# Fused causal attention and two expert layers: the attention stage rewritten as a pipeline over heads with one written order for TensorE

## Chip, cores and metric

One core of a Trainium2 chip. The metric is the device time of one execution in microseconds (us). The kernel before took 442.41 us, the median of three runs from 440.71 to 443.2.

## The reference

Inputs: q, k, v of 2 batches, 8 heads, 576 rows and 64 columns, and a vector s per head. For each head:

```python
scores = scale * np.matmul(q, k.transpose(0, 1, 3, 2))
cum = np.cumsum(np.maximum(s, 0.0), axis=-1)
bias = -(cum[:, :, :, None] - cum[:, :, None, :])
scores = np.where(causal, -1000000000.0, scores + np.minimum(bias, 0.0))
scores = scores - np.max(scores, axis=-1, keepdims=True)
attn = np.exp(scores)
attn = attn / (np.sum(attn, axis=-1, keepdims=True) + 1e-09)
return np.matmul(attn, v)
```

The 1152 rows of 512 that come out go through a layer of 8 experts (top one by a gate, with a capacity), and its result through a second layer of 8 experts with another gate and a bias. The change touches the attention stage alone.

## The kernel before, in words

**Tiling.** Heads are worked in eight pairs p (two heads i = 0, 1 of one batch b, pair hp of four). The 576 query rows of a head are cut into five tiles t of 64, 128, 128, 128 and 128 rows (`ROWS`, starting at `QS`); tile t sees keys 0 to w = 64, 192, 320, 448 or 576. Tile 0 is called the 64-row tile.

**Operands, `load(p)` (L272 to L311).** One transfer brings q and k of a pair, transposed, into `qkd`, twice over the 128 partitions; others bring rows of the cumulated s into `kb` and `qb` and the values into `vt`. A score is made of rounded numbers and their remainders: ScalarE casts q to `qa` and k to `ka` (L306, L308), VectorE casts q to the upper half of `qb` (L307), and GpSimd (VectorE for the first pair) subtracts to get the remainders `qa` and `kb` (L309, L310). `load(p + 1)` is called at the start of pair p. The transfers are issued on SyncE's queue; `qkd`, `qa` and `ka` have two buffers, as have `qb` and `kb`.

**Scores (L355 to L377).** For each head and tile, TensorE makes `ps` out of two products, `qa` by `ka` (L364) and `qb` by `kb` (L366), and adds the causal mask on the diagonal block as a bfloat16 product of an identity and a matrix `later` (L369). Tile 4, 576 wide, is made in two halves of 288, in two PSUM banks. Each bank holds one piece. VectorE reads it, scales it and takes the running minimum (L372) into `sc` (three buffers); ScalarE takes the exponential and its row sum (L376) into `ebuf[t, i]`.

**Transposes (L378 to L387).** TensorE turns the exponentials in blocks of 128 columns (L383) into PSUM tiles `pt`, and VectorE (L385) or ScalarE (L387) copies them to `eT`. For the second head of a pair both copies of tile 4 are ScalarE's. The 64-row tile is turned as a 64-row block.

**Values and rows (L434 to L483).** When both heads are turned, TensorE multiplies the values by `eT` into `pa` (columns 0 to 320) and `pb` (320 to 576), the two heads in the two halves of the columns of the array (L441). ScalarE and VectorE copy them to `xu`; ten products with an identity and the gate's weights (L454) turn them into rows `px`; VectorE scales these by the inverse row sums (L457, L467), and SyncE stores them to `x1` (`keep_rows`). Pairs 4 and 7 also route their batch (`route`).

**PSUM.** `pss` has four banks for `ps`, `pst` four for `pt`, `pa`, `pb`, `px` and the router's tiles.

**Order.** The program is written tile by tile, but a scheduler chooses the order on each engine by what it thinks is ready; that order is then fixed. So scores of a pair come to stand among transposes and value products of the one before. `tc.issue_after(x)` makes the instructions under it come after x in that order, `tc.keep_in_program_order` and `behind` keep an instruction's place. The expert layers that follow have an order written by hand; the first of their gathers reads the stored rows.

Of the kernel before, what the change touches and what calls it, by code (L numbers as in the profile page):

```python
# [6 lines left out]
F32 = mybir.dt.float32  # L7
# [10 lines left out]
NT = 5  # L18
# [63 lines left out]
def build(tc, ctx, spots, tab, qk, v, s, wg, wa, cap, mod, wg2, mb, wb, out):  # L82
# [108 lines left out]
    with ExitStack() as actx:  # L191
# [13 lines left out]
        later = ae.tile([P, P], BF16, name="later")  # L205
        nc.gpsimd.memset(later, 0.0)
        nc.gpsimd.affine_select(out=later, in_=later, pattern=[[-1, P]], compare_op=ALU.is_ge, fill=-8.0e9,
                                base=0, channel_multiplier=1)
# [10 lines left out]
        for t in range(NT):  # L219
            for j in range(2):  # L220
                et = ae.tile([P, P * (t + 1)], F32, name=f"e{t}_{j}")
                nc.gpsimd.memset(et[:, 64 + P * t:P * (t + 1)], 0.0)
                ebuf[t, j] = et
# [48 lines left out]
        def load(p):  # L272
# [8 lines left out]
            vt = ap.tile([P, NT, 2 * D], F32, name="vt")  # L281
# [37 lines left out]
        ahead = load(0)  # L319

        for b in range(B):
            for hp in range(4):
                p = 4 * b + hp
                qa2, ka2, qb2, kb2, vt = ahead
                if p < 7:
                    ahead = load(p + 1)
                if p == 0:
                    with tc.issue_after(operands[-1]):
                        nc.gpsimd.memset(wgid[:, :, P:DW], 0.0)
                        filled = nc.gpsimd.tensor_copy(wgid[:, :, 0:P], ident.unsqueeze(1).to_broadcast([P, 4, P]))  # L330
                    behind(ctab, tab)
                    wgv = wg.rearrange("(hp two d) e -> two d hp e", two=2, d=D)
                    for i in range(2):
                        behind(wgid[64 * i:64 * i + 64, :, P + E * i:P + E * i + E], wgv[i])
                if p > 3:
                    for i in range(2):
                        first.append(fetch(wa, 0, 2 * (p - 4) + i, pin=True))
                if p == 3:
                    for i in range(2):
                        xc = const.tile([H1, 2, RW], F32, name=f"xc{i}")  # L340
                        with tc.issue_after(filled.ins):
                            nc.gpsimd.memset(xc, 0.0)
                        xcs.append(xc)
                    zrow = ac.tile([P, 1, DM], F32, name="zrow")
                    with tc.issue_after(filled.ins):
                        nc.gpsimd.memset(zrow, 0.0)
                    tc.keep_in_program_order(nc.sync.dma_start(
                        out.rearrange("(p t) d -> p t d", t=9), zrow.to_broadcast([P, 9, DM])))
                eTs = []
                for i in range(2):  # L350
                    h = 2 * hp + i
                    qa, ka, qb, kb = qa2[:, i], ka2[:, i], qb2[:, i], kb2[:, i]
                    eT = ap.tile([P, NT, S], F32, name="eT", bufs=3)
                    eTs.append(eT)
                    for t in range(NT):  # L355
                        r = ROWS[t]
                        w = QS[t] + r
                        q0 = QS[t]
                        sc = ap.tile([P, S], F32, name="sc", bufs=3)
                        low = 3.0e38  # L360
                        for c0, c1 in ((0, w // 2), (w // 2, w)) if w > 512 else ((0, w),):
# [100 lines left out]
                if p == 7:  # L462
                    exp = route(1)
# [743 lines left out]
```

## Time and profile before

| what | value |
|---|---|
| median of 3 runs | 442.41 us |
| the profiled execution | 439.67 us |
| its span, first to last instruction | 437.9 us |
| TensorE busy (matmul) | 411.4 us, 94% |
| VectorE busy | 198.6 us, 45% |
| ScalarE busy | 170.5 us, 39% |
| GpSimd busy | 130.4 us, 30% |
| mean granted TensorE clock | 0.973 |

Times in the trace count from the first instruction of the span. Busy shares are means over all stages: attention, about the first 125 us, and the expert layers after it. [...] L12 is line 12 of the kernel before.

### The profile page before, as it was taken

The page shows a single profiled execution, that of the slowest core. Times are in us where ns is not written, and L with a number is a line of the kernel's source. Part 1 is how long each engine was busy: PE and PEld are TensorE (multiplying, and loading weights), DVE is VectorE, ACT ScalarE, POOL GpSimd, SP SyncE. Part 2 cuts the span into 40 slices and gives each one's busy share as a digit, 9 for nine tenths or more (in the row PEclk, how much of TensorE's full clock was granted, in tenths as well). Part 3 has the DMA queues.
Part 4 walks back from the last instruction along what each step waited for, and adds up shares of the span by engine and source line. Part 5 has one row for each costly group of instructions (what it writes and reads, how often), then busy time and mean ns, then how long its engine had stood idle before and what let it go on. Part 6 is the DMA issues. An engine that isn't in the chain of part 4 may idle for free.

```text
span 437.9 us, 8869 instructions
## 1 busy us (share of the span) xinstructions
PE 411.4 (94%) x3193; PEld 371.9 (85%) x3193; DVE 198.6 (45%) x782; ACT 170.5 (39%) x452; POOL 130.4 (30%) x154
## 2 busy tenths in 40 slices
PE   4997999999987999999999999999999999999980
PEld 1775777788757999998999999998999999999980
DVE  7779878998671032232322315176912243111110
ACT  5776888876531121212121212146313364131220
POOL 4397444330018220020110100323464447030120
PEclk8889999999998999999999999999999999999995
DMA  3846279343324766676768696994149646010010
GB/s 113 309 115 207 75 252 325 100 158 127 102 107 128 248 194 209 198 241 210 252 201 294 189 305 208 271 310 160 36 108 361 214 135 207 21 40 16 7 41 23
DMA packets 30580, 74.64 MB, mean 170 GB/s; under 512 B 9196, under 2 KB 11628, under 8 KB 30526
## 3 DMA queue, kind: packets, MB, share of 16 engines
q1 hardware_dynamic: 24190, 66.75, 45.8%
q0 software_dynamic: 6336, 7.22, 6.0%
q8 instruction: 27, 0.44, 0.4%
q14 instruction: 27, 0.22, 0.2%
HBM read 63.78 MB, written 10.51 MB: 170 GB/s over the span
## 4 chain that ended last, share of the span: by engine, by line
PE 58%; DVE 5%; DMA 3%; issue 2%; ACT 1%; POOLq 0%; POOL 0%; DVEq 0%
PE ps L657 32%; PE ps L665 6%; PE ps L667 6%; PE ps L666 6%; PE pty L732 3%; PE ptx L642 2%; PE p L748 1%; DMA st<-in_wb 1%; DMA yc<-y,idx 1%; DVE lo L577 1%; DVE pos L173 1%; DMA xc<-x,list 1%; DVE hidden L723 0%; ACT hi L575 0%; POOLq L835 0%
## 5 line engine op out<-in xcount | busy, mean ns | idle before, releaser
L657 PE MATMUL ps<-xn,st 128*128 128x160 f32 (+7 forms) x576 | 83.6, 299 | 0.0
L657 PE MATMUL ps<-hidden,st 128*128 128x160 f32 (+7 forms) x576 | 81.8, 296 | 0.0
L657 PEld LDWEIGHTS ps<-xn,st 128*128 128x128 f32 x576 | 77.7, 193 | 1.9 <-ACT yT L709 1.1
L657 PEld LDWEIGHTS ps<-hidden,st 128*128 128x128 f32 x576 | 76.3, 190 | 0.6
L710 DVE COPY yT<-ps 128x276 f32<-128x276 f32 (+8 forms) x26 | 9.2, 353 | 98.6 <-ACT yT L709 98.6
L376 ACT ACTIVATE e<-sc,nmx 64x64 f32<-64x64 f32 (+4 forms) x80 | 44.6, 560 | 15.2 <-DVE sc L372 8.3
L364 PE MATMUL ps<-ka,qa 128*64 128x64 f32 (+2 forms) x96 | 35.8, 380 | 6.4 <-DVE qa L309 4.5
L709 ACT COPY yT<-ps 128x276 f32<-128x276 f32 (+8 forms) x26 | 8.2, 316 | 79.1 <-PE ps L657 48.7
L665 PE MATMUL ps<-hidden,hi 128*128 128x276 f32 x128 | 38.2, 299 | 0.6 <-DVE hidden L723 0.6
L665 PE MATMUL ps<-xs,hi 128*128 128x276 f32 x128 | 38.4, 300 | 0.0
L601 POOL DMA_INDIRECT xc<-x,idx x14 | 13.9, 994 | 80.3 <-DVE eq L770 77.4
L383 PE MATMUL pt<-ident,e 128*128 128x128 f32 (+1 forms) x240 | 36.8, 282 | 1.0 <-DVE eT L385 0.9
L666 PE MATMUL ps<-hidden,hi 128*128 128x276 f32 x128 | 37.1, 290 | 0.2 <-DVE hidden L723 0.2
L666 PE MATMUL ps<-xs,hi 128*128 128x276 f32 x128 | 37.1, 290 | 0.0
L667 PE MATMUL ps<-hidden,lo 128*128 128x276 f32 x128 | 37.1, 290 | 0.0
L667 PE MATMUL ps<-xs,lo 128*128 128x276 f32 x128 | 37.1, 290 | 0.0
L372 DVE TENSOR_SCALAR_CACHE_REDUCE sc<-ps 64x64 f32<-64x64 f32 (+4 forms) x80 | 32.9, 422 | 6.8 <-PE ps L369 3.9
L309 POOL TENSOR_TENSOR qa<-qkd,qb 64x576 fp32r<-64x576 f32 x14 | 20.5, 1462 | 38.8 <-ACT qa L306 38.2
L577 POOL TENSOR_TENSOR lo<-st,hi 128x512 fp32r<-128x512 f32 x16 | 22.3, 1401 | 32.7 <-ACT hi L575 32.6
L824 POOL DMA_INDIRECT out<-yr,oi x13 | 15.6, 1201 | 53.8 <-ACT yr L733 49.2
L383 PEld LDWEIGHTS pt<-ident,e 128*128 128x128 f32 (+1 forms) x240 | 26.9, 143 | 4.9 <-DVE eT L385 1.1
L366 PE MATMUL ps<-kb,qb 128*64 128x64 f32 (+2 forms) x96 | 29.1, 310 | 0.6 <-POOL kb L310 0.6
(275 smaller groups left out, 779.8 us busy)
## 6 DMA issues: line engine op xcount, KB each, us to landing
st<-in_wa SPq DMA_DIRECT2D x64, 512.0 KB
st<-in_wb SPq DMA_DIRECT2D x24, 512.0 KB
qkd<-in_qk SPq DMA_DIRECT2D x6, 1152.0 KB
y<-yr SPq DMA_DIRECT2D x8, 390.0 KB
vt<-in_v SPq DMA_DIRECT2D x8, 320.0 KB
qkd<-in_qk SPq DMA_DIRECT2D x4, 576.0 KB
out<-zrow SPq DMA_DIRECT2D x1, 2304.0 KB
x<-xrow SPq DMA_DIRECT2D x2, 768.0 KB
```

The source lines that it names most:

```text
L309: eng.tensor_tensor(qa[64:128, i], qd[64:128], qb[64:128, i].bitcast(F32), op=ALU.subtract)
L364: nc.tensor.matmul(o, qa[:, q0:q0 + r], ka[:, c0:c1], start=True, stop=False, skip_group_check=True)
L366: nc.tensor.matmul(o, qb[:, q0:q0 + r], kb[:, c0:c1], start=False, stop=c1 <= q0, skip_group_check=True)
L372: nc.vector.tensor_scalar(sc[:r, c0:c1], o, -0.125, low, op0=ALU.mult, op1=ALU.min, accum_out=nmx[:r])
L376: nc.scalar.activation(e[:r, :w], sc[:r, :w], AF.Exp, bias=nmx[:r], scale=-1.0, accum_out=rsum[:r, b, t, h:h + 1])
L383: nc.tensor.transpose(pt[:, j - g0, :r], e[:r, j * P:(j + 1) * P], ident[:r, :r])
L577: eng.tensor_tensor(lo[:, c:c + h], st[:, c:c + h], hi[:, c:c + h].bitcast(F32), op=ALU.subtract)
L657: pin(nc.tensor.matmul(out[:, 0:c], w[:, o:o + P], mv, start=first, stop=last, skip_group_check=True))
L665: pin(nc.tensor.matmul(out[:, 0:c], hi, mv[:, 0, :], start=first, stop=False, skip_group_check=True))
L666: pin(nc.tensor.matmul(out[:, 0:c], hi, mv[:, 1, :], start=False, stop=False, skip_group_check=True))
L667: pin(nc.tensor.matmul(out[:, 0:c], lo, mv[:, 0, :], start=False, stop=last, skip_group_check=True))
L824: put = nc.gpsimd.indirect_dma_start(out=out, out_offset=bass.IndirectOffsetOnAxis(ap=oi[:, i:i + 1], axis=0), in_=yr[:, i, :], in_offset= ...
```

## The change

The attention stage is written as 17 steps. Step n makes the scores of head n and, between them, the transposes of head n - 1: bank 0 (tiles 2 and 1), transposes of tiles 1 and 2, bank 1 (tiles 3 and 0), transposes of tiles 3 and 0, banks 2 and 3 (the halves of tile 4), transposes of tile 4. After each even step from 2 on come the value products of the pair just turned, all of them; after each odd step from 3 on the pair's rows (`close_pair`). Every TensorE instruction of this goes through `pe`, which puts it behind the one before it. The two tiles of a shared bank get one mask: a 256-column one for tiles 2 and 1, a 192-column one for tiles 3 and 0. The transposes of the 64-row tile take the full 128 rows of a buffer that is filled with zeros at the start. The rounding of q for `qb` goes to GpSimd for pairs 2 to 7. `vt` has three buffers (before: two), `eT` two (before: three).

```diff
-        later = ae.tile([P, P], BF16, name="later")
+        later = ae.tile([P, P + 64], BF16, name="later")
         nc.gpsimd.memset(later, 0.0)
...
-                nc.gpsimd.memset(et[:, 64 + P * t:P * (t + 1)], 0.0)
+                nc.gpsimd.memset(et[:, 64 + P * t if t else 0:P * (t + 1)], 0.0)
...
-            vt = ap.tile([P, NT, 2 * D], F32, name="vt")
+            vt = ap.tile([P, NT, 2 * D], F32, name="vt", bufs=3)
...
-                    nc.vector.tensor_copy(qb[64:128, i], qd[64:128])
+                    (nc.gpsimd if p > 1 else nc.vector).tensor_copy(qb[64:128, i], qd[64:128])
...
+        def pe(op, *args, **kw):
+            with tc.issue_after(order[-1]) if order else ExitStack():
+                ins = op(*args, **kw)
+            order[:] = [ins.ins]
+            return ins
...
+        def scores(h, bank):
...
+            ps = pss.tile([P, 512], F32, name="ps")
+            for t, o0, c0, c1 in bank:
+                r, q0 = ROWS[t], QS[t]
+                o = ps[:r, o0:o0 + c1 - c0]
+                pe(nc.tensor.matmul, o, qa[:, q0:q0 + r], ka[:, c0:c1], start=not o0, stop=False, skip_group_check=True)
+                pe(nc.tensor.matmul, o, qb[:, q0:q0 + r], kb[:, c0:c1], start=False, stop=c1 <= q0,
+                   skip_group_check=True)
+            t, o0, c0, c1 = bank[0]
+            if t == 2:
+                masked = ps[:, P:512].rearrange("p (u c) -> p u c", u=2)[:, :, 64:192]
+                mask = later[:, 0:P].unsqueeze(1).to_broadcast([P, 2, P])
+            elif t == 3:
+                masked, mask = ps[:, 320:512], later
+            else:
+                masked, mask = ps[:, QS[4] - c0:c1 - c0], later[:, 0:P]
+            if c1 > QS[t]:
+                pe(nc.tensor.matmul, masked, identb, mask, start=False, stop=True, skip_group_check=True)
+            for t, o0, c0, c1 in bank[::-1]:
...
+                nc.vector.tensor_scalar(h.sc[t][:r, c0:c1], ps[:r, o0:o0 + c1 - c0], -0.125, low, op0=ALU.mult,
+                                        op1=ALU.min, accum_out=h.nmx[t][:r])
...
+        def turned(h, t):
...
+            r, e = ROWS[t], ebuf[t, h.i]
+            for g0, g1 in [(0, t + 1)] if t < 4 else [(0, 3), (3, 5)]:
+                pt = pst.tile([P, 4, P], F32, tag="t", name="pt")
+                for j in range(g0, g1):
+                    pe(nc.tensor.transpose, pt[:, j - g0, :], e[:, j * P:(j + 1) * P], ident)
...
+        BANKS = ((2, 0, 0, 320), (1, 320, 0, 192)), ((3, 0, 0, 448), (0, 448, 0, 64)), ((4, 0, 0, 288),), ((4, 0, 288, 576),)
+        filled = None
+        for n in range(2 * 2 * 4 + 1):
+            before = heads[n - 1] if n else None
+            if n < 16:
+                if n % 2 == 0:
+                    open_pair(n // 2)
+                open_head(pairs[-1], n % 2)
+            for banks, tiles in (((0,), (1, 2)), ((1,), (3, 0)), ((2, 3), (4,))):
+                for x in banks if n < 16 else ():
+                    scores(heads[n], BANKS[x])
+                for t in tiles if before else ():
+                    turned(before, t)
...
+            if n > 1 and n % 2 == 0:
+                values(pairs[n // 2 - 1])
+            if n > 2 and n % 2:
+                close_pair(pairs[n // 2 - 1])
+        close_pair(pairs[7])
```

`open_pair(p)` takes over the loads of pair p and calls `load(p + 1)` with what stood at a pair's start before; `values(k)` holds L434 to L449 and `close_pair(k)` L450 to L483, as they were, with their matmuls through `pe`. What the router does with matmuls does not go through it.

## Rows read from the trace of the kernel before

**Rows 1.** Busy time by stretch; columns: stretch, length, busy PE, PEld, DVE, ACT, POOL, clock, DMA
```profile
43.50:110.20 66.70, 66.70 (x548) 53.40 (x547) 56.69 (x234) 52.70 (x164) 22.99 (x17) 1.00 0.50 172
110.20:123.50 13.30, 13.30 (x122) 10.47 (x122) 6.89 (x24) 6.22 (x19) 0.00 (x0) 1.00 0.44 147
```

**Rows 2.** Waits of TensorE from 10 to 124 us
```profile
PE ps L364 <- DVE sc L372: 1.6, 2, 0.9
PE pt L383 <- DVE eT L385: 0.9, 1, 0.9
```

**Rows 3.** TensorE in order of time, value products and rows; columns: start us, length, instruction
```profile
56.65 1.20 PE L441 MATMUL pa<-eT,vt 128*64 128x320 f32 x12
57.78 0.41 PE L364 MATMUL ps<-ka,qa 128*128 128x320 f32 x1
...
58.34 1.96 PE L441 MATMUL pb<-eT,vt 128*64 128x256 f32 x20
60.23 0.47 PE L364 MATMUL ps<-ka,qa 128*128 128x448 f32 x1
...
110.20 1.20 PE L441 MATMUL pa<-eT,vt 128*64 128x320 f32 x12
...
113.74 1.49 PE L454 MATMUL px<-wgid,xu 128*128 128x144 f32 x10
115.17 4.13 PE L383 MATMUL pt<-ident,e 64*128 64x64 f32 x30
119.22 1.20 PE L441 MATMUL pa<-eT,vt 128*64 128x320 f32 x12
...
122.09 1.49 PE L454 MATMUL px<-wgid,xu 128*128 128x144 f32 x10
123.42 0.28 PE L252 MATMUL pr<-oh,ones 128*128 128x40 bf16 x5
```

**Rows 4.** TensorE in order of time, scores of tiles 4, 0 and 1
```profile
60.78 0.38 PE L364 MATMUL ps<-ka,qa 128*128 128x288 f32 x1
...
61.13 0.29 PE L364 MATMUL ps<-ka,qa 128*128 128x288 f32 x1
...
61.40 0.23 PE L369 MATMUL ps<-later,identb 128*128 128x128 bf16 x1
61.44 0.22 PE L364 MATMUL ps<-ka,qa 128*64 128x64 f32 x1
...
67.22 0.24 PE L364 MATMUL ps<-ka,qa 128*64 128x64 f32 x1
...
67.60 0.36 PE L364 MATMUL ps<-ka,qa 128*128 128x192 f32 x1
...
67.98 1.15 PE L383 MATMUL pt<-ident,e 128*128 128x128 f32 x9
```

**Rows 5.** TensorE in order of time, transposes with and without the 64-row tile
```profile
63.30 0.64 PE L383 MATMUL pt<-ident,e 64*128 64x64 f32 x3
63.70 0.34 PE L364 MATMUL ps<-ka,qa 128*128 128x192 f32 x1
...
65.00 0.50 PE L383 MATMUL pt<-ident,e 128*128 128x128 f32 x3
65.25 0.38 PE L364 MATMUL ps<-ka,qa 128*128 128x288 f32 x1
```

**Rows 6.** Groups of instructions by line from 0 to 130 us; count, busy us, mean ns, idle before
```profile
L309 POOL TENSOR_TENSOR qa<-qkd,qb 64x576 fp32r<-64x576 f32 x14 | 20.5, 1462 | 38.8 <-ACT qa L306 38.2 <-PE ps L369 0.6
L330 POOL COPY wgid<-ident 128x512 f32<-128x512 f32 x1 | 0.6, 607 | 0.1
L307 DVE CAST qb<-qkd 64x576 fp32r<-64x576 f32 x16 | 10.1, 638 | 0.9 <-DMA qkd<-in_qk 0.4
L306 ACT CAST qa<-qkd 128x576 fp32r<-128x576 f32 x16 | 10.7, 667 | 3.6 <-POOL qa L309 1.7 <-issue 1.1 <-DMA qkd<-in_qk 0.8
L387 ACT COPY eT<-pt 128x256 f32<-128x256 f32 (+3 forms) x48 | 19.4, 411 | 11.6 <-PE pt L383 11.6
```

More of the change, by code (lines that the diff above doesn't have):

```diff
@@ new lines, in build, with open_pair @@
+        order = []
+        def pe(op, *args, **kw):
[3 more added lines that the diff above has]
+            return ins
+        class Part:
+            pass
+        loads, pairs, heads = {0: load(0)}, [], []
+        xrows = []
+        def open_pair(p):
+            nonlocal filled
+            pr_ = Part()
+            pr_.p, pr_.b, pr_.hp, pr_.eTs = p, p // 4, p % 4, []
+            pr_.qa, pr_.ka, pr_.qb, pr_.kb, pr_.vt = loads.pop(p)
+            pairs.append(pr_)
+            if p < 7:
+                loads[p + 1] = load(p + 1)
+            if p == 0:
+                with tc.issue_after(operands[-1]):
+                    nc.gpsimd.memset(wgid[:, :, P:DW], 0.0)
+                    filled = nc.gpsimd.tensor_copy(wgid[:, :, 0:P], ident.unsqueeze(1).to_broadcast([P, 4, P]))
+                behind(ctab, tab)
+                wgv = wg.rearrange("(hp two d) e -> two d hp e", two=2, d=D)
+                for i in range(2):
+                    behind(wgid[64 * i:64 * i + 64, :, P + E * i:P + E * i + E], wgv[i])
+            if p > 3:
+                for i in range(2):
+                    first.append(fetch(wa, 0, 2 * (p - 4) + i, pin=True))
+            if p == 3:
+                for i in range(2):
+                    xc = const.tile([H1, 2, RW], F32, name=f"xc{i}")
+                    with tc.issue_after(filled.ins):
+                        nc.gpsimd.memset(xc, 0.0)
+                    xcs.append(xc)
+                zrow = ac.tile([P, 1, DM], F32, name="zrow")
+                with tc.issue_after(filled.ins):
+                    nc.gpsimd.memset(zrow, 0.0)
+                tc.keep_in_program_order(nc.sync.dma_start(
+                    out.rearrange("(p t) d -> p t d", t=9), zrow.to_broadcast([P, 9, DM])))
@@ new lines, in values @@
+        def values(k):
+            pa = pst.tile([P, 320], F32, tag="t", name="pa")
+            pb = pst.tile([P, 256], F32, tag="t", name="pb")
+            for po, lo, hi in ((pa, 0, 320), (pb, 320, 576)):
+                js = [j for j in range(NT) if max(P * j, lo) < hi]
+                for j in js:
+                    c0 = max(P * j, lo)
+                    for i in range(2):
+                        pe(nc.tensor.matmul, po[64 * i:64 * i + 64, c0 - lo:hi - lo], k.vt[:, j, D * i:D * i + D],
+                           k.eTs[i][:, j, c0:hi], start=(j == 0), stop=(j == js[-1]), skip_group_check=True)
+            k.xu = ap.tile([P, S], F32, name="xu")
+            nc.scalar.copy(k.xu[:, 0:320], pa)
+            nc.vector.tensor_copy(k.xu[:, 320:576], pb)
+            k.rinv = ap.tile([P, NT, 2], F32, name="rinv")
+            nc.vector.tensor_scalar_add(k.rinv, rsum[:, k.b, :, 2 * k.hp:2 * k.hp + 2], 1.0e-9)
+            nc.vector.reciprocal(k.rinv, k.rinv)
```

260 lines of the change are left out of this document (100 added, 160 removed).

## The prediction

> **What bounds the kernel now.** I read the busy time by stretch first [rows 1]. In the five pairs of the middle stretch TensorE is busy for all of 66.7 us at the full granted clock, ScalarE for 52.7 and VectorE for 56.69; in the last 13.3 us of attention TensorE is never idle either. So from 43.5 on attention is TensorE's time. I read TensorE's waits next [rows 2]: 1.6 us on VectorE's reads of scores and 0.9 on one of its copies. Since TensorE is never idle from 43.5 us on, both lie ahead of that. Then I read TensorE's instructions in order of time, where the distance between the starts of two groups is what the first cost, switches included [rows 3 to 5]. The value products of one pair start at 56.65 and those of the fourth pair after it at 110.20: 13.39 us per pair. What follows attention (routing, then the experts) starts when the last pair is done, and the change does not touch it, so a microsecond off attention is one off the kernel.
>
> **What the change does to TensorE's instructions.** No product is left out, so gains come from switches between array shapes, shorter chains and fewer waits.
>
> (a) Transposes of the 64-row tile. Today they take the array as 64*128. A group of three with one of them lasts 0.40 us (63.30 to 63.70), three full ones 0.25 (65.00 to 65.25) [rows 5]: 0.15 dearer. Entering costs more: ten products before such a group last 1.43 us (113.74 to 115.17), before a full-size matmul 1.33 [rows 3]. After the change all are 128*128. 0.25 x 16 heads = -4.0 us; where the entry is paid by another switch anyway only 0.15, -2.4.
>
> (b) Scores of the 64-row tile. Today 0.38 us (67.22 to 67.60) [rows 4], its own 64*64 mask included. After: the same two products, then a mask shared with the 448-wide tile, full size. The mask's shape is not in the trace; I take off the change of shape around it, the size of (a)'s entry: 0.11 x 16 = -1.8. Ends: nothing, and 0.15, -2.4.
>
> What the row shows at the other end of this tile: the full-size mask before it starts 0.04 us ahead of it (61.40, 61.44) [rows 4], so entering the 64-column form costs nothing visible. [...]
>
> (c) One mask for tiles 1 and 2. Tile 1 today takes 0.38 (67.60 to 67.98). The second half of tile 4, which follows another score without a mask between, needs 0.31 with its mask although it is 288 wide against 192 [rows 4]. Inside a shared bank I take 0.30: 0.08 x 16 = -1.3; ends 0 and -1.9.
>
> (d) The halves of tile 4 stand together. Together, the first costs 0.35 (60.78 to 61.13) and the second 0.31 with a mask of about 0.04 (as 61.40 to 61.44): 0.08 is saved when nothing comes between. Today something does in a part of the heads; I take half of the 16: -0.6; ends 0 and -1.3.
>
> (e) Value products in one piece. Today mostly two: 1.13 (56.65 to 57.78) plus 1.89 (58.34 to 60.23), 3.02 us; whole, 2.87 (119.22 to 122.09) [rows 3]. With the switch on entering the second piece (0.10) this is 0.25 a pair. The last pair's is whole already, seven are cut: -1.8; ends seven times 0.15, -1.1, and seven times 0.35, -2.5, where some are in three pieces.
>
> Sum of (a) to (e): -4.0 - 1.8 - 1.3 - 0.6 - 1.8 = -9.5 us. As a check from the other side I put a pair together from the best spacings: scores per head 0.55 for the 448-wide tile (60.23 to 60.78), 0.66 for tile 4, 0.45 for the 320-wide (between the 288 and the 448), 0.30 for tile 1 and 0.27 for the 64-row one, so 2.2; transposes 15 x 0.107 = 1.6 (between the 0.083 of three when a score follows and the 0.135 of the run of 30 from 115.17 to 119.22); twice that, plus 2.87 and 1.33, is 11.8 against 13.39: 1.6 x 8 = -12.8. The difference of 3.3 is what the list does not name, above all switches between scores, transposes and products, of which the new order has a fixed few. I take -11, the middle; the far end is -12.8.
>
> **What it does to waits.** (f) The q casts of pairs 2 to 7 leave VectorE: 0.638 mean, 1.28 a pair [rows 6]. VectorE is not last in the middle stretch, so nothing there. Ahead of it VectorE's lateness costs TensorE 2.5 us [rows 2]; the casts of pairs 2 and 3 go from there, and transposes now come one head after their exponentials. I take -1.5; ends 0 and -2.5.
>
> (g) On GpSimd a cast lies between a copy of 128x512 at 0.607 and a subtraction of the same 64x576 at 1.46 [rows 6]; I take 0.75, nearer the copy because it too reads one operand. A pair then costs GpSimd 4 x 1.46 + 2 x 0.75 = 7.3 us (8.8 at worst) of a period near 12. Operands are made a pair ahead, so this is hidden; without that cover a pair's first score would wait for 2.2 to 2.9 us. Everything behind the casts on GpSimd (subtractions, fills) moves back by up to 1.5, and the queue of SyncE, whose next q and k load waits for the last subtraction, by the same. Pieces of rows are stored about a head later; only the gather after attention reads them, and the last store's place is unchanged.
>
> (h) Fixed order at the start. Today, while head 2's operands are being made, TensorE does work of heads 1 and 2 in turns. In the new order head 1's transposes stand behind head 2's first scores. Bounds: 0, and two subtractions, 2.9; I take +1.5, in the middle, because step 1 offers 3.8 us of other work first (2.2 and 1.6, above).
>
> (i) New waits in the steady part. Each copy out of PSUM has about half a step until its buffer is wanted, scores a whole step. ScalarE is at 52.70 / 5 = 10.5 us a pair [rows 1], VectorE at 11.3 less 1.3 = 10.0: both fit in 12, but not loosely. Ends 0 and 1.4 a pair; I take 0.2 for seven pairs, +1.4, near the end that [rows 1] show today (none).
>
> (j) The end. Pair 7's transposes want the PSUM buffers of pair 6's last products, and the last copy of values is exposed as now: +0.5; ends 0 and +1.3. The wider mask fill, the larger zero fill and the other buffer counts cost nothing: GpSimd does the fills before the first scores, and idles afterwards until pair 1's operands.
>
> Total: -11 - 1.5 + 1.5 + 1.4 + 0.5 = -9.1 us. The profiled execution took 439.67 (span 437.9 and 1.8 around it), so it would take 430.6; it stands 0.6% under the median of 442.41, to which the same difference gives 433.3.
>
> **Rivals.** One, slower: the value products wait for ScalarE. They now stand right behind the transposes of the odd head's last tile, both of whose copies are ScalarE's; the second part of the products needs them 1.1 us later, when the first is done. ScalarE's four operand casts of a pair (0.67 each) may stand ahead of them in its queue: 2.7 us. The wait is then 2.7 + 2 x 0.41 - 1.1 = 2.4 a pair [rows 6], 19 in all: in the place of the 1.4 of (i), -10.5 + 19 = +8.5, 450.9 us. It decides above 1.3 us a pair. For it: ScalarE is at 10.5 of 12. Against it: the copies become ready early in a step in which it has little else that is due, and today ScalarE waits 11.6 us for the transposes that it copies [rows 6], not they for it.
>
> Two, no change: buffers and order cost 1.4 us a pair in many small waits (score reads behind row scaling and copies on VectorE, four PSUM buffers for eight uses a step), seven pairs: -10.5 + 9.8 = -0.7, 441.7. For it: today's order was fitted to readiness, and where VectorE was loaded most, TensorE waited for it. Against it: a whole head's slack.
>
> Three, the shapes give less: a change of shape costs the same wherever it stands and shared banks save nothing; (a) at -2.4, (b) and (c) at 0, the rest as above, and nothing beyond the list: -11 becomes -4.8, the total -2.9, 439.5. This is also the case in which the change does not do what it says to the array.
>
> **How the numbers follow.** Forecast 0.68, rival one 0.09, two 0.12, three 0.11. 0.5%, 2.2 us, is about what a measurement here can tell from no change. Faster 0.79 (forecast and three), same 0.12, slower 0.09. The range: from the far end of the products and waits without new ones (-12.8 - 1.5 = -14.3 from 442.4, 428) up to 440, which takes in three and most of the bounds of (h) to (j), and leaves out one and most of two.
>
> **What would show it.** Right: starts of one pair's value products 11.8 to 12.4 us apart, each 2.87 in one piece; 64-row transposes as cheap as others; attention's end near 115; VectorE without q casts after pair 1; the stretch after attention as long as before. Wrong: TensorE rows waiting on ScalarE's copies at the value products in pair after pair (one), on VectorE's score reads or copies (two), groups of the same length as today (three), or a lower granted clock beyond 25 us.

## The result, and the profile after

The changed kernel took 434.45 us, the median of 4 runs (433.49 to 435.36), beside 441.56 us (440.52 to 443.2, 4 runs) for the kernel before: a ratio of 0.983, 95% interval 0.9806 to 0.9854. The forecast was 433.3 us, range 428 to 440. All ratios and intervals here are of fast runs; one run of e6_order_alone and two of e9_before_gpsimd_setup were slow, and without them the medians of these two are 437.51 and 439.36 us.

| what | before | after |
|---|---|---|
| the profiled execution | 439.67 us | 435.36 us |
| its span | 437.9 us | 433.5 us |
| TensorE busy (matmul) | 411.4 us | 400.5 us |
| VectorE, ScalarE, GpSimd busy | 198.6, 170.5, 130.4 us | 190.9, 169.1, 137.3 us |
| mean granted TensorE clock | 0.973 | 0.977 |
| router's first product, the end of attention | 123.42 us | 117.72 us |

Attention ends 5.7 us sooner. What follows takes 314.5 us before and 315.8 after; over the fourteen profiles of this document it lies between 313.8 and 317.2, whatever was done in attention, so nothing is read from that difference.

The order of time on TensorE, where the value products of a pair and the rows of the pair before are the marks (columns as in [rows 3], which these lines answer to):

```profile
68.08 1.33 PE L327 MATMUL pa<-eT,vt 128*64 128x320 f32 x10
69.11 0.38 PE L327 MATMUL pb<-eT,vt 128*64 128x256 f32 x1
...
71.19 0.42 PE L327 MATMUL ps<-ka,qa 128*128 128x320 f32 x1
...
74.76 1.39 PE L327 MATMUL px<-wgid,xu 128*128 128x144 f32 x10
...
79.53 1.33 PE L327 MATMUL pa<-eT,vt 128*64 128x320 f32 x10
...
113.52 1.20 PE L327 MATMUL pa<-eT,vt 128*64 128x320 f32 x12
114.55 1.91 PE L327 MATMUL pb<-eT,vt 128*64 128x256 f32 x20
116.39 1.49 PE L327 MATMUL px<-wgid,xu 128*128 128x144 f32 x10
117.72 0.28 PE L253 MATMUL pr<-oh,ones 128*128 128x40 bf16 x5
```

From 68.08 to 79.53 is one pair: 11.45 us, where [rows 3] gave 13.39 on average. It is made of the value products, 3.11 us to 71.19, a step of 3.57 to the rows at 74.76, the rows, and a step of 3.64. The last pair's value products, at the bottom, take 2.87 (113.52 to 116.39). Both of these recur below.

Within a step (answers to [rows 4, 5]; the lengths overlap, 0.19 us at 61.43 with the next start 0.03 later, so a cost is read between starts):

```profile
60.94 0.45 PE L327 MATMUL ps<-ka,qa 128*128 128x448 f32 x1
61.23 0.36 PE L327 MATMUL ps<-kb,qb 128*128 128x448 f32 x1
61.43 0.19 PE L327 MATMUL ps<-ka,qa 128*64 128x64 f32 x1
61.46 0.22 PE L327 MATMUL ps<-kb,qb 128*64 128x64 f32 x1
61.52 0.26 PE L327 MATMUL ps<-later,identb 128*128 128x192 bf16 x1
61.61 0.71 PE L327 MATMUL pt<-ident,e 128*128 128x128 f32 x5
62.08 0.38 PE L327 MATMUL ps<-ka,qa 128*128 128x288 f32 x1
```

The 64-row tile's scores with the shared mask cost 0.18 us (61.43 to 61.61), where [rows 4] had 0.38; five transposes, the 64-row one among them, cost 0.47 (61.61 to 62.08).

The waits of TensorE from 10 to 124 us (answers to [rows 2]; of those left out, one is the wait for the first operands, ahead of all this, and the others lie in the router or are 0.5 or less):

```profile
PE pt L327 <- DVE xu L434: 1.9, 2, 1.6
PE px L327 <- DVE eT L418: 1.5, 2, 1.1
PE ps L327 <- POOL kb L311: 1.2, 1, 1.2
...
PE ps L327 <- POOL qa L310: 0.9, 1, 0.9
PE pa L327 <- ACT eT L420: 0.8, 1, 0.8
PE pt L327 <- DVE sc L403: 0.8, 1, 0.8
```

With the 0.5 for `pb` and the small ones the waits between 11 and 47 us sum to 7.5. Before they were 3.4: the 2.5 of [rows 2], and 0.8 for head 2's operands, which [rows 2] left out. From 47 us to the seventh pair's value products only 0.6 is left. So the change gained in the steady pairs and lost at the start: the second pair's value products begin at 44.09 after, 43.49 before.

What VectorE did meanwhile (in order of time; in brackets the idle time before a line and what ended it):

```profile
29.88 0.15 DVE L506 CAST capf<-capi 128x1 f32<-128x1 int32 x1 [3.43 <-DMA capi<-in_cap]
32.14 0.21 DVE L522 CAST modf<-modi 128x10 f32<-128x10 int32 x1 [2.10 <-DMA modi<-in_mod]
32.38 1.39 DVE L527 TENSOR_SCALAR sel<-modf 128x5 f32<-128x5 f32 x2
33.69 0.41 DVE L434 COPY xu<-pb 128x256 f32<-128x256 f32 x1
```

VectorE stood still for 5.5 us in front of two casts of a few numbers, whose loads had not landed, and the copy `xu` and the score reads stood behind them. The diff doesn't touch these casts (in the kernel before they are L406 and L422). Whether they explain the lost time is what the first group of experiments asks. The second asks which part of the change brought the gain.

### The profile page after: what moved, and what is told of

Its sections match the earlier page's. It is cut to its first block, busy times and chain, and to the rows that moved or that the text cites. A ratio compares the mean times of both kernels' runs of the same rounds, so it can differ in the third digit from the quotient of the medians.

```text
span 433.5 us, 8785 instructions
## 1 busy us (share of the span) xinstructions
PE 400.5 (92%) x3161; PEld 371.8 (86%) x3161; DVE 190.9 (44%) x770; ACT 169.1 (39%) x452; POOL 137.3 (32%) x167
## 4 chain that ended last, share of the span: by engine, by line
PE 58%; DVE 5%; DMA 3%; issue 2%; ACT 1%; POOLq 0%; POOL 0%; DVEq 0%
PE ps L711 32%; PE ps L719 6%; PE ps L721 6%; PE ps L720 6%; PE pty L786 3%; PE ptx L696 2%; PE p L802 1%; DMA yc<-y,idx 1%; DMA st<-in_wb 1%; DVE lo L631 1%; DVE pos L173 1%; DMA xc<-x,list 1%; DVE hidden L777 0%; ACT hi L629 0%; POOLq L889 0%
## 5 line engine op out<-in xcount | busy, mean ns | idle before, releaser
L407 ACT ACTIVATE e<-sc,nmx 128x192 f32<-128x192 f32 (+4 forms) x80 | 44.7, 561 | 13.2 <-DVE sc L403 13.1
L327 PE MATMUL pt<-ident,e 128*128 128x128 f32 x240 | 36.1, 280 | 3.3 <-DVE xu L434 1.9
L327 PE MATMUL ps<-ka,qa 128*128 128x320 f32 (+2 forms) x96 | 32.5, 345 | 5.9 <-DVE qa L310 5.0
L403 DVE TENSOR_SCALAR_CACHE_REDUCE sc<-ps 128x192 f32<-128x192 f32 (+4 forms) x80 | 31.6, 416 | 4.5 <-PE ps L327 3.7
L327 PEld LDWEIGHTS pt<-ident,e 128*128 128x128 f32 x240 | 27.3, 144 | 4.8 <-DVE xu L434 2.3
L327 PE MATMUL ps<-kb,qb 128*128 128x320 f32 (+2 forms) x96 | 25.7, 306 | 1.2 <-POOL kb L311 1.2
L770 ACT ACTIVATE hidden<-ps 128x160 f32<-128x160 f32 (+7 forms) x36 | 10.5, 292 | 40.8 <-PE ps L711 37.5
```

The source lines that it names most:

```text
L327: ins = op(*args, **kw)
L403: nc.vector.tensor_scalar(h.sc[t][:r, c0:c1], ps[:r, o0:o0 + c1 - c0], -0.125, low, op0=ALU.mult, op1=ALU.min, accum_out=h.nmx[t][:r])
L407: nc.scalar.activation(ebuf[t, i][:r, :w], h.sc[t][:r, :w], AF.Exp, bias=h.nmx[t][:r], scale=-1.0, accum_out=rsum[:r, k.b, t, n:n + 1])
L770: relu = nc.scalar.activation(k.hs[:, 2 * j], k.b[:, 0], AF.Relu)
```

## The experiments

Twelve kernels ran. Each is the changed kernel with one edit, unless said otherwise. "Pairs 2 to 7" is the mean distance from the second value products to the seventh (five pairs), "3 to 5" from the third to the fifth, two pairs in which TensorE shows no wait above 0.03 us, except in e8; the end is the router's first product.

| label | median us (runs) | ratio to before, 95% interval | pairs 2 to 7 | 3 to 5 | end |
|---|---|---|---|---|---|
| before | 441.56 (4) | | 13.34 | 13.11 | 123.42 |
| after | 434.45 (4) | 0.983, 0.9806 to 0.9854 | 11.91 | 11.44 | 117.72 |
| e1_late_setup | 436.13 (6) | 0.9882, 0.9845 to 0.9918 | 11.88 | 11.44 | 117.53 |
| e2_q_vector | 436.12 (6) | 0.9883, 0.9847 to 0.9919 | 11.84 | 11.64 | 117.17 |
| e3_t0_rows64 | 436.36 (6) | 0.989, 0.9854 to 0.9926 | 12.07 | 11.78 | 119.64 |
| e4_own_banks | 436.73 (6) | 0.9878, 0.9836 to 0.9919 | 12.21 | 11.92 | 118.72 |
| e5_after_again | 435.36 (6) | 0.9846, 0.9811 to 0.988 | 11.85 | 11.44 | 119.09 |
| e6_order_alone | 437.96 (6) | 0.9916, 0.9885 to 0.9947 | 12.58 | 12.52 | 119.68 |
| e7_gpsimd_setup | 430.17 (6) | 0.9736, 0.9705 to 0.9767 | 11.90 | 11.43 | 113.99 |
| e8_free_order | 440.14 (12) | 0.9973, 0.995 to 0.9996 | 13.73 | 13.40 | 122.25 |
| e9_before_gpsimd_setup | 439.59 (12) | 0.9948, 0.9913 to 0.9983 | 13.68 | 13.60 | 123.66 |
| e10_values_split | 434.33 (6) | 0.9843, 0.9802 to 0.9884 | 11.98 | 11.70 | 117.95 |
| e11_head2_vector | 431.84 (6) | 0.9761, 0.9715 to 0.9808 | 11.90 | 11.44 | 113.66 |
| e12_load2_late | 429.4 (6) | 0.9729, 0.969 to 0.9768 | 11.90 | 11.44 | 113.08 |

e5 is the changed kernel once more:

> The changed kernel once more, so that the other kernels of this call stand beside it. Both theories: 434 to 436 us, pairs 11.4 to 11.6 us apart from the third to the sixth, attention ends at 117.5 to 118.

Its pairs 3 to 5 agree with the first profile to 0.01 us; its end is 1.4 us later (117.5 to 118 was expected), and all of that arises ahead of 47 us, where TensorE's granted clock differs (0.84 from 25 to 47 us, 1.00 in the first profile; last section). So distances of steady pairs can be compared to some hundredths, ends of single profiles only to about 1.5 us.

### The start: who stands in VectorE's queue

**e1_late_setup.** The setup (the two casts and the ten operations that make the biases; the expectations below count ten in all, the edits move twelve) stands behind the second pair's value products.

```diff
-                nc.vector.tensor_copy(capf, capi[:, 0:1])
...
+            if n == 5:
+                setup = tc.issue_after(pairs[1].turned)
+                setup.__enter__()
+                nc.vector.tensor_copy(capf, capi[:, 0:1])
...
```

> Two theories of why TensorE waits 5.4 us for VectorE's work between 25 and 47 us in the changed kernel, where the kernel before waits 2.6. Queue theory: VectorE stands still for 3.4 us and then 2.1 us in front of two small casts of the setup whose loads have not landed (the capacity and the modality), with score reads and copies behind them. This kernel puts VectorE's setup work two pairs later. Queue theory: the stand-still at 26 to 32 us is gone, TensorE's waits between 25 and 47 us fall to 1.5 us or less, and the kernel takes 3.5 to 4.5 us less than the changed one: about 430.5 us. Rival, contention: VectorE is late there because GpSimd is busier and its small operations on SBUF stall; then the waits stay above 3 us at this place or come back where the setup is put, and the time stays within 1 us of the changed kernel, 433.5 to 435.5 us.

Of the 5.4 us of waits that the expectation puts down to VectorE, the rows give it 3.9 and ScalarE 1.5. The stand-still at 26 to 32 us went, and the end stayed: 117.53. One new wait took the place of the old ones. First VectorE's order of time, then TensorE's:

```profile
37.58 0.10 DVE L524 CAST capf<-capi 128x1 f32<-128x1 int32 x1
37.65 1.29 DVE L525 CAST modf<-modi 128x10 f32<-128x10 int32 x1
38.98 1.39 DVE L530 TENSOR_SCALAR sel<-modf 128x5 f32<-128x5 f32 x2
...
40.79 0.23 DVE L530 TENSOR_SCALAR sel<-modf 128x5 f32<-128x5 f32 x2
...
41.35 0.20 DVE L535 TENSOR_TENSOR bias<-bias,t 128x40 f32<-128x40 f32 x1
41.47 0.35 DVE L403 TENSOR_SCALAR_CACHE_REDUCE sc<-ps 128x192 f32<-128x192 f32 x1
```

```profile
42.72 1.40 PE L327 MATMUL pt<-ident,e 128*128 128x128 f32 x5 [4.73 <-DVE sc L403]
```

The loads had landed by then; twelve small operations in one block, 37.58 to 41.5, were enough, since the score reads and a copy that TensorE's next transposes need stand behind them. So the wait for the loads was not the whole cause: here 4 us of VectorE in one piece did as much. And the rival has its part: the wait came back where the setup was put, as it said, and 2.7 of the 4 us are two of the rows above, drawn out beside GpSimd's subtractions (1.29 and 1.39 us; the like of the second took 0.23 at 40.79).

**e7_gpsimd_setup.** The twelve operations go to GpSimd, behind the fourth pair's operands.

```diff
+            if n == 5:
+                setup = tc.issue_after(operands[-1])
+                setup.__enter__()
+                nc.gpsimd.tensor_copy(capf, capi[:, 0:1])
...
-                nc.vector.tensor_copy(modf, modi[:, :, :, 0])
+                nc.gpsimd.tensor_copy(modf, modi[:, :, :, 0])
...
```

> The ten small operations that turn the capacity and the modalities into biases move from VectorE to GpSimd, behind the operands of the fourth pair. Theory (in the first 47 us VectorE stood in its queue for the loads that feed them, and with it the score reads and copies that TensorE wants; moving them as one block on VectorE only moved the wait): the waits of TensorE between 25 and 47 us go from 5.4 to under 2 us, the period from the second to the third value products goes below 12.2, attention ends at 113.5 to 115, 431 to 432.5 us. Rival (the time between 25 and 47 is set by the operands of the third and fourth pair, by GpSimd and the loads): attention ends at 117 to 118.5, and the waits stand at the same places with other names; 434 to 436 us.

430.17 us, 5.2 below e5, which ran beside it; the intervals of the two don't meet. (Against the first four runs of the changed kernel it is 4.3, and attention ends 3.7 sooner than in the first profile, 0.6 of it gained ahead of the first value products.) All waits of TensorE between 25 and 47 us that are left:

```profile
27.72 0.92 PE L327 MATMUL pa<-eT,vt 128*64 128x320 f32 x7 [2.00 <-ACT eT L420]
39.22 0.52 PE L327 MATMUL pt<-ident,e 128*128 128x128 f32 x3 [0.79 <-DVE sc L403]
39.92 0.44 PE L327 MATMUL pt<-ident,e 128*128 128x128 f32 x2 [0.19 <-ACT eT L420]
42.74 1.95 PE L327 MATMUL pb<-eT,vt 128*64 128x256 f32 x18 [0.49 <-ACT eT L420]
```

Every wait for VectorE but one is gone, and the second value products come 15.44 us after the first, where e5 took 20.64 (6.7 us of waits from 11 to 47 us against 5.6 in e7, and a stretch at a granted clock of 0.50, from 39 to 43 us, behind the longest). Three of the expected numbers were missed: the time is below its range, the waits sum to 3.5, not under 2 (the 2.0 at the first value products stayed, as in e5), and the next pair takes 12.55, not under 12.2. The theory holds on the end, 113.99, and its rival falls: the pairs from 47 us on take what they took, so the 4 to 5 us come from the setup's place on VectorE. How much of them is the wait for loads, and how much the drawn-out operations, was not separated.

**e9_before_gpsimd_setup.** The same move in the kernel before, at its third pair, to see whether the setup had been a cost all along.

```diff
-                    nc.vector.tensor_copy(modf, modi[:, :, :, 0])
...
+                if p == 2:
+                    setup = tc.issue_after(operands[-1])
+                    setup.__enter__()
+                    nc.gpsimd.tensor_copy(capf, capi[:, 0:1])
+                    nc.gpsimd.tensor_copy(modf, modi[:, :, :, 0])
...
```

> The kernel before, with the ten small operations for the biases on GpSimd, as in the run e7_gpsimd_setup, and nothing else changed. Theory (they hurt the changed kernel because its VectorE met them 2 to 4 us before their loads had landed, and its TensorE may do nothing else meanwhile; in the kernel before they stood behind work that had landed and the scheduler's order had other things to do): under 1.5 us gained, the second value products at 16 to 17 us after the first, 440 to 441.5 us. Rival (some 4 us of VectorE's time near the start cost either kernel the same): the attention ends 3 to 4 us earlier, 437.5 to 438.5 us.

The end stays, 123.66 against 123.42. But the setup did cost the kernel before something: with it gone from VectorE TensorE's waits from 25 to 47 us fall from 2.6 to 1.0, and the second value products come 15.69 us after the first (16 to 17 expected, 16.98 before). VectorE's and TensorE's rows of the kernel before, first the one and then the other:

```profile
37.72 1.45 DVE L427 TENSOR_SCALAR sel<-modf 128x5 f32<-128x5 f32 x2
```

```profile
39.51 0.40 PE L364 MATMUL ps<-ka,qa 128*128 128x288 f32 x1 [0.91 <-DVE sc L372]
```

The next pair takes the gain back (14.48 us, 13.17 before). The median is 1.5 lower than that of the kernel before beside it (441.05), which the end of attention does not account for; 439.59 lies below the theory's range. So most of the 4 to 5 us are a price of the change, an order that can't go round a late engine; up to 1.5 of them the kernel before may have paid too.

**e11_head2_vector and e12_load2_late**, both on top of e7, go after the next two waits: the second pair's first head gets its subtractions on VectorE, and ScalarE's casts for the third pair stand behind the last copy of head 1.

```diff
-                eng = nc.gpsimd if p else nc.vector
+                eng = nc.gpsimd if p > 1 or p and i else nc.vector
```

```diff
-                with tc.issue_after(summed.ins):
+                with tc.issue_after(copied[-1] if p == 2 else summed.ins):
                     nc.scalar.copy(qa[:, i], qd)
...
```

> The biases on GpSimd (as in e7_gpsimd_setup) and, for the second pair's first head, the two subtractions on VectorE in GpSimd's place. Theory (TensorE, held to its order, waits 0.91 and 1.18 us for these two, at 18.9 and 20.5 us): 1 to 2 us of that go, the attention ends at 112 to 113, 428 to 429.5 us. Rival (VectorE is then late with the score reads and copies of head 1, or the next wait, 2.0 us for ScalarE's last copy, grows by as much): the end stays at 113.5 to 114.5, 429.5 to 431 us.

> As e11_head2_vector, and ScalarE's four casts for the third pair (2.7 us) stand behind the last copy of head 1 instead of ahead of it. Theory (they stand ahead of it at 24.5 to 27.2 us, and TensorE waits 2.0 us with the first value products for that copy): 1.5 to 2 us of that go too, the attention ends at 110.5 to 112, 426.5 to 428.5 us. Rival (the third pair's operands come 2 to 3 us later and TensorE waits for them at head 4): the end stays where e11_head2_vector has it, 428 to 430 us.

In e11 the two waits for head 2's operands became 0.53 and 1.89 us, 2.4 in the place of 2.1, now for VectorE's subtractions: the rival, though 431.84 lies above both ranges. In e12 the 2.0 us at the first value products went, but these came at 26.76 instead of 24.96: head 2's waits are 0.3 of that, and from 22 to 26 us the granted clock was at 0.50 to 0.75 where e7 had 1.00. The end is 0.9 sooner than in e7. 429.4 and 430.17 can't be told apart; either is faster than both kernels.

### The steady pairs: shapes, banks or order

**e3_t0_rows64, e4_own_banks, e2_q_vector** each undo one part: 64-row transposes; a bank and a mask for each tile; q cast on VectorE for all pairs.

```diff
-                    pe(nc.tensor.transpose, pt[:, j - g0, :], e[:, j * P:(j + 1) * P], ident)
+                    pe(nc.tensor.transpose, pt[:, j - g0, :r], e[:r, j * P:(j + 1) * P], ident[:r, :r])
```

```diff
-        BANKS = ((2, 0, 0, 320), (1, 320, 0, 192)), ((3, 0, 0, 448), (0, 448, 0, 64)), ((4, 0, 0, 288),), ((4, 0, 288, 576),)
+        BANKS = ((2, 0, 0, 320),), ((1, 0, 0, 192),), ((3, 0, 0, 448),), ((0, 0, 0, 64),), ((4, 0, 0, 288),), ((4, 0, 288, 576),)
...
```

```diff
-                    (nc.gpsimd if p > 1 else nc.vector).tensor_copy(qb[64:128, i], qd[64:128])
+                    nc.vector.tensor_copy(qb[64:128, i], qd[64:128])
```

> Undoes one part: the transposes of the 64-row tile take 64 rows of the array again, all else as changed. Prediction term (a): 0.25 us a head, 4.0 us slower than the changed kernel, 438.5 us; 2.4 us if its entry is paid by another switch anyway. If a change of the array's shape is hidden in the new order, no difference: 434.5 us. In the steady stretch the value products of successive pairs would stand 11.9 to 12.0 us apart, not 11.45.

> Undoes one part: each tile's scores have a bank and a mask of their own again (six banks a head, five masks), in the same written order. Prediction terms (b) and (c): 0.11 + 0.08 us a head, 3.1 us slower than the changed kernel, 437.5 us. If the gain is in the order alone: no difference, 434.5 us. If the four score banks then become short, with six uses a step, TensorE shows waits on VectorE's score reads in the steady stretch and it is 5 us or more slower.

> Undoes one part: q is rounded by VectorE for all pairs again. Steady stretch: VectorE is not the bound, so the value products of successive pairs stay 11.4 to 11.8 us apart. If contention with GpSimd is the cause of the waits between 25 and 47 us, this kernel is 2 us or more faster than the changed one (432.5 or less). If the queue behind the setup's loads is the cause, the waits stay, VectorE has 1.3 us more per pair, and the time is 434 to 437 us.

Against 11.44 the two clean pairs are 0.34 us longer with 64-row transposes (0.45 to 0.55 expected), 0.48 with banks of their own (0.38), 0.20 with q on VectorE. The ends and medians move by less than these profiles can tell. The 0.20 is one pair alone: e2's value products start at 55.06, 66.86 and 78.34, so the first of the two pairs takes 11.80 and the second 11.48; over pairs 2 to 7 e2 is even 0.07 shorter. Its early waits stay, too (4.6 us from 25 to 47 us, 5.4 in the changed kernel), so the cast's place explains neither those nor the gain.

**e6_order_alone** has all three edits; the written order and the value products in one piece are left.

> Only the written order and the value products in one piece are left: q is cast on VectorE, the 64-row transposes read 64 rows, and every tile has a bank and a mask of its own. If the parts add up (0.33 us per pair from the transposes, 0.47 from the banks, each measured alone against the changed kernel), pairs start 11.45 + 0.80 = 12.25 us apart, attention ends near 121, and 1.14 of the 1.94 us per pair that the change saved are the written order's own; 438 to 439.5 us. Rival, that the shapes matter only because TensorE is the engine that all wait for (something else takes over when it gets slower, or the scheduler fills the gaps): under 12 or over 12.6 apart.

12.52 apart, 1.08 above the changed kernel, where e3 and e4 sum to 0.82: at the edge of the rival. The rows show what the difference is. Two of the value products in the steady pairs of e6:

```profile
67.04 1.20 PE L327 MATMUL pa<-eT,vt 128*64 128x320 f32 x12
79.56 1.20 PE L327 MATMUL pa<-eT,vt 128*64 128x320 f32 x12
```

Twelve in 1.20 us, as in the kernel before and in the last pair of the changed one; the steady pairs of the changed kernel have ten in 1.33 before the first of `pb`. The start of one such group in the changed kernel, one group each of e3 and e4, and the start of one in the kernel before:

```profile
68.08 0.48 PE L327 MATMUL pa<-eT,vt 128*64 128x320 f32 x1
```

```profile
69.33 1.20 PE L327 MATMUL pa<-eT,vt 128*64 128x320 f32 x12
```

```profile
67.34 1.20 PE L327 MATMUL pa<-eT,vt 128*64 128x320 f32 x12
```

```profile
56.65 0.49 PE L441 MATMUL pa<-eT,vt 128*64 128x320 f32 x2
```

The first and the last of these lines are each of a window of 0.3 us: in the changed kernel one product starts in it, in the kernel before two, 0.007 us apart. The two heads' products lie in the two halves of the array's columns and run side by side; in the changed kernel's clean pairs the second head's starts 0.25 us late, and for so long the first runs alone. What ScalarE does then (its order of time):

```profile
67.54 0.56 ACT L407 ACTIVATE e<-sc,nmx 128x320 f32<-128x320 f32 x1
67.99 0.20 ACT L407 ACTIVATION_READ_ACCUMULATOR e<-sc,nmx 128x1 f32 x1
68.08 0.20 ACT L420 COPY eT<-pt 128x64 f32<-128x64 f32 x1
```

The copy of the second head's 64-row tile ends at 68.28, and the late product starts 0.05 us behind it. It does so at the third, fourth and fifth value products of after, e1, e5, e7, e11 and e12; at the sixth it is 0.08 us late, at the last two not at all. In e3, e4 and e6, where TensorE comes a little later, the copy has been done for 0.1 to 0.7 us and the two start together. So in three pairs of the changed kernel 0.25 us goes to a wait for ScalarE, and the parts save TensorE more than e3 and e4 show: 0.34 + 0.25 = 0.59 for the transposes, 0.48 + 0.25 = 0.73 for the banks, together 1.32, against 1.08 + 0.25 = 1.33 from e6. The cast's 0.20, which e6 has undone as well, is left out of this sum, because it stood in one pair of e2 and e6's clean pairs are even (12.51 and 12.52); with it in, the three parts sum to 1.02 without any late half, also near 1.08. The rows favour the first reading: the value products take 2.87 in e3, e4 and e6, so the loss outside them is 0.58, 0.72 and 1.32. The late start itself is read from the rows of eight kernels; a kernel with that copy taken off ScalarE was not tried.

**e8_free_order** keeps shapes, banks and program text, and drops the chain.

```diff
-            with tc.issue_after(order[-1]) if order else ExitStack():
-                ins = op(*args, **kw)
-            order[:] = [ins.ins]
-            return ins
+            return op(*args, **kw)
```

> The changed kernel with its shapes, banks and program order, but without the chain that holds TensorE to one order: the scheduler orders its instructions again. Theory (of the 1.94 us per pair, some 1.1 come from the order: whole blocks of transposes and scores, value products not mixed in): pairs 12.3 to 12.8 apart, the attention ends at 119 to 123, 436 to 441 us. Rival (the order was given by the program's text anyway, and the shapes and banks are what saved the time): pairs 11.4 to 11.7 apart, within 1 us of the changed kernel, and the start may even be shorter, since head 2 needn't be waited for.

440.14 us, ratio 0.9973: nearly all of the gain is gone, with every shape and bank of the change still there. Pairs 2 to 7 take 13.73 (12.3 to 12.8 expected); 2.4 us of waits lie in these five pairs (one is below), and without them it is 13.25, near the kernel before's 13.34. The rival falls: the text's order alone does not bring it.

```profile
61.33 1.51 PE L326 MATMUL pb<-eT,vt 128*64 128x256 f32 x12 [2.08 <-ACT eT L417]
```

So neither half works by itself as the sum suggests: the order without the shapes gives 0.76 us a pair (13.34 to 12.58), the shapes without the order about 0.1 with e8's waits taken out and a loss of 0.4 with them in, both together 1.43. The scheduler's order in e8 is another one than in the kernel before, so the 0.1 is a comparison of two orders as well.

**e10_values_split** cuts the value products in two, the second part behind the next head's first bank of scores.

```diff
-                values(pairs[n // 2 - 1])
+                values(pairs[n // 2 - 1], 0)
...
+                if banks == (0,) and n > 2 and n % 2:
+                    values(pairs[n // 2 - 1], 1)
```

> The changed kernel with the value products cut in two: the first 320 columns of a pair where they were, the other 256 behind the first bank of scores of the next head. Theory (in one piece they take 3.11 us in the steady pairs and 2.87 alone, the rest is the change of tile form on the way in and out, so a second way in and out costs about 0.24 us): pairs 11.6 to 11.8 us apart, the attention ends 1 to 2 us later, 435.5 to 437 us. Rival (the form changes are hidden and the one piece is worth nothing): pairs 11.4 to 11.5 apart, 434 to 435.5 us; the rival of the other sign: the second half waits less for ScalarE's last copy, the pairs with waits (the first ones) get shorter and the end comes up to 1 us sooner.

0.26 us per pair in the two clean pairs, the theory's number; its reason does not hold, since 3.11 against 2.87 is the late start shown above and not a change of form, so that the number agrees is luck. Over five pairs it is 0.07, and no difference in the median (434.33), since the distances around the waits fall otherwise. The two pieces in its order of time:

```profile
67.60 1.40 PE L327 MATMUL pa<-eT,vt 128*64 128x320 f32 x12
68.93 0.41 PE L327 MATMUL ps<-ka,qa 128*128 128x320 f32 x1
...
69.74 1.96 PE L327 MATMUL pb<-eT,vt 128*64 128x256 f32 x20
71.63 0.76 PE L327 MATMUL pt<-ident,e 128*128 128x128 f32 x5
```

1.33 and 1.89 us, 3.22 in all against 3.11 in one piece; the other 0.15 lies among the neighbours. The first piece carries the late start here too (0.21 us).

## Why the prediction was right, point by point

The time came out 1.2 us above the forecast, for reasons that are only half the forecast's, and the closeness is in part luck. Its sum for attention was -11 for the products and +1.9 for waits and the end, so -9.1, with the end near 115. The trace has -5.7, and the end at 117.72; the medians differ by 7.1, and the kernel before came out 0.9 below the 442.41 that the forecast started from. Early waits are 4.1 more (7.5 - 3.4), steady ones 0.6, late second halves some 1 us; so by difference the products took about 11.4 less, an estimate that puts all else at nothing.

**The products' sum: right in size.** It was worked out twice, as a list (-9.5) and from the best spacings (-12.8); what came, about -11.4, lies between, where it was put. The band of 11.8 to 12.4 us per pair was too high for the clean pairs (11.44) and right on average over five (11.91), which has the waits in it.

**Who earned it: wrong.** (a) to (c) were 0.88 us a pair, written as if each stood alone. Undone together they cost 1.08, or 1.33 without the late half: (a) 0.30 per head where 0.25 was put, (b) and (c) 0.36 where 0.19 was ((b) reckons with 0.11 for an entry that (a) reads as 0.10). The step that failed is the sentence that gave what the list doesn't name 1.5 us in all. e6 gives the order 0.76 a pair; (d) and (e), which are in it, were put at 0.3, and (d) was not tried by itself, so some 0.46 a pair is left, 3.7 in all. And e8 shows that without the order the shapes bring about 0.1. The rows gave prices of switches; they couldn't show that a scheduler which may mix again will mix again.

**(e), right in price, not in effect.** 0.25 a pair, e10 0.26; but the one piece takes 3.11, not 2.87, because of the late second half.

**The row on entering the 64-column form: right.** From the 448-wide tile's last product to the 64-column ones and on to the mask the starts are 0.20, 0.03, 0.06 and 0.09 apart. The first of these is the entry, and in e4, where a full-size mask follows that product, the step is 0.21 (47.92 to 48.13): the entry costs nothing visible here. Elsewhere a gap shows: at the value products, of the same 128*64 form, the first starts 0.20 us after the last transpose, where transposes follow each other at 0.11.

**(f), wrong in sign.** It took -1.5 for VectorE's relief at the start. e2 shows that the cast's engine decides nothing, and the early waits other than (h)'s grew by 2.8 (4.1 - 1.3), for the most part by the setup, which (f) didn't look at: it stands in VectorE's queue too, and nothing in the diff moves it. In the order of before its casts came at 32.10 and 35.58, with no wait for their loads. e7 has 2.0 us less of these waits than the first profile, and prices the setup's place at 5.2 us (3.7 by the ends of those two profiles). The 2.5 us that VectorE's lateness cost TensorE were the right row with the wrong owner: e9, with the q casts in place and the setup gone, has 1.0 us left of these waits from 25 us on. What was missing is the question which instructions of VectorE stand ahead of those late ones, and which the new order brings to the front.

**(g), right.** A q cast on GpSimd took 0.67 us (0.75 put), hidden:

```profile
L308 POOL CAST qb<-qkd 64x576 fp32r<-64x576 f32 x12 | 7.9, 667 | 16.9 <-PE ps L327 16.8
```

**(h), right.** 0.92 and 1.18 us of waiting for head 2's operands, where the kernel before waited 0.8: +1.3, and +1.5 was put. e11 shows that it isn't GpSimd's slowness alone, and the order alone doesn't make the wait: in e4 and e6 TensorE comes to head 2's scores at 21.03 and 20.04 instead of 17.97, finds the operands there, and the first value products come at 25.03 and 24.59, no later than the changed kernel's 25.60.

**(i), right in size.** 0.6 us of steady waits and some 1 us of late halves (0.25 in each of three pairs, less in others): 1.6, and 1.4 was put. The larger part is not a wait for a buffer, as (i) has it, but rival one's wait for ScalarE.

**(j), not what happened.** From the seventh value products to the end it takes 14.10 us (103.62 to 117.72), before 13.22: +0.9, and +0.5 was put. But TensorE is idle for 0.1 of the 14.10; the stretch is longer because all scores of the last head stand in it, where before only half of one tile's did (111.33 to 111.86). That work is part of the pairs' sum, so the wait that (j) puts at 0.5 measured 0.1.

**Rivals.** One named the right engine and a price ten times too high: the odd head's value products do wait for ScalarE in three pairs, 0.25 us and not 2.4, because only the second head's half waits, and for the 64-row tile's copy, not tile 4's. Two is out in the steady part; at the start TensorE does wait for score reads and copies, behind the setup. Three is out: shapes gave more than the list said, given the order.

## What to carry to other kernels

A written order for an engine takes away its way round a late neighbour, so with it goes a look at every instruction that the neighbours' queues bring up in the same stretch, setup and loads included; here twelve operations on 1 to 40 columns cost 4 to 5 us beside some 11 that the products gained. Test the parts of a change both alone and left out: cheaper shapes were worth about 0.1 us a pair under the scheduler's order, waits left out, and 0.7 under the written one. And read the first microsecond of a group of products that run side by side: a late half shows as no idle time.

## What the runs showed of the hardware

**Half-array products ran side by side, each from when its own data were there.** Two products in the two column halves start 0.007 us apart (the kernel before at 56.65) and cost the time of one (the next two start 0.32 later, and so does the next one of the half that starts alone); when one is 0.25 us late the group takes 0.24 longer (3.11 against 2.87), and the views of waits used here don't list it, since the engine is busy.

**Tiny VectorE operations took longer beside GpSimd's subtractions.** In e1 two operations on 128x5 took 1.39 us together (38.98) while GpSimd was subtracting, and two of the same form 0.23 later (40.79), between subtractions:

```profile
38.84 1.41 POOL L310 TENSOR_TENSOR qa<-qkd,qb 64x576 fp32r<-64x576 f32 x1
```

In the changed kernel they took 1.39 (32.38) beside a subtraction of 1.40 (32.27). What draws them out no run here shows.

**Behind some waits the granted clock was lower.** In e5 TensorE waited 2.04 us for VectorE up to 35.17, and the granted clock was then 0.56 from 37 to 39 us, 0.50 from 39 to 43 and 0.73 from 43 to 45. In the first profile of the same kernel the wait at that place was 1.63 us and the clock was 1.00 from 25 to 47 us; in e1 it was 0.50 from 43 to 46, behind the 4.73. In e8, with a wait of 2.23 us up to 37.11, the mean from 25 to 47 us was 0.84; in e7, with the 2.00 at the first value products, it was 1.00. In e4 a 320-wide score product at 46.36, 4.9 us behind a wait of 2.52, lasted 0.41 us, as in the first profile at a clock of 1.00 (0.42 at 71.19); in e5 one at 40.33, 5.2 us behind the 2.04, lasted 0.64. Windows of e5 (length, busy PE, PEld, DVE, ACT, POOL, then the clock):

```profile
33.00:35.00 2.00, 0.12 (x2) 0.00 (x0) 1.74 (x4) 0.00 (x0) 1.68 (x2) 1.00 0.44 142
...
39.00:41.00 2.00, 1.70 (x7) 1.63 (x7) 2.00 (x11) 2.00 (x5) 0.60 (x2) 0.50 0.95 265
```

So e7's gain over e5 is made of waits and of a stretch at half clock that followed one of them; whether the wait brought it on is not shown, and how the 5.2 us divide was not measured.
